# Gated linear attention feeding a mixture of attention experts: outputs of one 128-token window and the state growth of the next as one task, with a reordered end, a narrower mask product and 128-token first projections

## The chip, the cores and the metric

One Trainium2 chip, one core. The metric is the device time of one execution in microseconds (us), lower is better; the kernel before was timed in 3 runs. Five engines run side by side, each in the order in which its instructions were written: PE (matrix products; PEld is its loading of weights), DVE (vector), ACT (scalar functions and copies), POOL (a second, slower vector engine) and SP (here only issues DMAs). They wait for each other through semaphores.

## What is computed

The reference, cut to what matters (B=4, heads H=8, S=768 tokens, D=48; then E=4 experts of width 64 over 384 features):

```python
f = sigmoid(f_logit)
for t in range(S):                                   # gated linear attention (GLA), per head
    state = f[t][:, None] * state + outer(k[t], v[t])
    y[t] = q[t] @ state
x = y as (B, S, 384)
logits = x @ w_gate; the two best experts get softmax weights w
for e in range(E):                                   # each expert: causal attention over all 768 tokens
    q, k, v = x @ wq[e], x @ wk[e], x @ wv[e]
    a = softmax(causal(q @ k.T / 8))
    out += w[e] * (a @ v @ wo[e])                    # 0 where e is not among the two
```

## The kernel before

All work is cut into tasks (`Order.add`): each has a kind, the engines that can run it with a planned cost, a function that emits its instructions, the tasks it needs, and the buffers it takes and uses. `Order.run` is a list scheduler that runs when the program is built: it keeps a planned clock for each engine, takes the task that can start first (ties by `place - AHEAD[kind]`), picks the engine, and so writes down one fixed order for every engine. `AHEAD`, `PLACES`, `WINDOW_AT`, `STICK` are the numbers that steer it. None of this costs anything on the chip; what counts there is the order.

**GLA windows** (`gla_window`, line 315): 24 windows of 128 tokens (`n`), six for each batch element. A window loads f, k, q as one block `fkq` (672 KB, line 341; three buffers) and v; ACT takes exp and log of f (L348, L349), DVE the running sum (L354), ACT two more exps (L360, L361), DVE scales k and q (L364, L365). Then PE has four tasks: `kt` (transposes of k, L371; evicted by ACT or DVE as task `gev`), `d` (the growth of the state, L392; it needs that eviction, and the `y` of the window before, through `state[2]`), `a` (scores within 64-token chunks and the part of the output that crosses chunks, L440, L430; evicted to `xs`) and `y` (outputs, L463, L430; it needs `xs` after POOL has masked it, L453). x is written in two parts, high (task `x`, a copy) and low (L482), since the products after it run as three float32r products of high and low parts (`mm3`, L509 to L511). Six small DMAs for a unit (`fill`, L230) move rows of x between partitions.

**Units** (`plan`, line 858): 8 units `u` of 384 tokens, two for each batch element (h = 0, 1). A unit projects x to q and k of two expert pairs (`proj_qk`) and to v and the gate's logits (`proj_v`), then for each pair runs the attention in groups of 128 query tokens (`experts`): scores `s` (L641, plus a causal mask added as a product of a constant with an identity, L645), row maxima on DVE (L657, L661), exp on ACT (L672), the inverse sum on DVE (L678, L679), scaling by POOL (`scale`, L692), transposes `tr` on PE (L702) with copies back (`pt`), and `attend`: the product with v (`av`, L727) and its two copies `zz`. `out_proj` (L748) multiplies by wo, an eviction and a DMA (L933) store 128 tokens. For h = 1 the three groups have 512, 640 and 768 keys, in that order.

The PE runs these tasks in four tilings, which the code calls modes: q (64x64 quarters: `a`, `y`, `d`), h (row halves: `s`), c (column halves: `av`), f (the full array: the rest). The planner charges 93 ns for a change of mode (`CHANGE`). In the first 95 planned us it also puts dummy products (L204) into the gaps it foresees on PE.

The first unit is special: its projections start in two pieces, tokens 0 to 255 and 256 to 383 (`for a, e, ws in ((0, 256, (0, 1)), (256, 384, (2,)))`). Its weights are loaded into four staging buffers `pp` (line 286) and split into high parts (L290 on POOL, or L225 on ACT) and low parts (L295 on DVE).

Of the kernel before, what the change touches and what calls it, by code (L numbers as in the profile page):

```python
# [16 lines left out]
B, H, S, D = 4, 8, 768, 48  # L17
# [26 lines left out]
CHANGE = 93  # L44
SEEN = {"PE": 190, "V": 125, "A": 145, "P": 65, "S": 0}
# [7 lines left out]
    "oev": 85.8, "out": -104.5, "w": -92.5, "wl": -13.5, "flag": 4.9,  # L53
}
STICK = 0
WINDOW_AT = (-0.27, -0.09, 0.18)
# [3 lines left out]
PLACES = {"w": 4.27, "hv": 11.3, "a0": 1.47, "a1": 4.16, "o": 3.45, "at": 23.67, "second": 0.71, "units": 1.53, "gate": 9.81, "wa": 0, "wo": 1.3}  # L60


def acopy(n):
    return 52 + 0.833 * n
# [144 lines left out]
class Kernel:  # L209
# [105 lines left out]
    def gla_window(self, o, n, x, state):  # L315
# [62 lines left out]
        old, sdone, before = state  # L378
# [17 lines left out]
        gr = o.add("d", [("PE", 240 if last_w else 460)], grow, [kev, lv, before], alloc=grown, uses=[ktb, vb], modes=("q", "q"))  # L396
# [61 lines left out]
        def outputs(e):  # L458
            for p in range(NP):
                for c in range(2):  # L460
# [7 lines left out]
        y = o.add("y", [("PE", 470 + (230 if w else 115))], outputs, [sel, lv],  # L468
                  alloc=([x] if w % 3 == 0 else []), uses=[xsb, vb, fkq, x, mid, ab] + ([old] if w else []),
                  modes=("q", "q"))  # L470
        y.spare, y.free = lambda: [ab.t[:, i, 0:NP * C] for i in range(2)], ev
        state = state[:2] + (y,)
# [8 lines left out]
        hi = o.add("x", [("A", acopy(512)), ("V", dcopy(512))], lambda e: self.copy(e, xout(0), yin()), [y], uses=[ab, x])  # L481
        lo = o.add("x", [("V", dcopy(512))], lambda e: nc.vector.tensor_sub(xout(1), yin(), xout(0)), [hi], uses=[ab, x])  # L482
        self.sums += [cm, t2]
        return lo, state
# [115 lines left out]
    def experts(self, o, ts, h, pr, group, first, place):  # L600
# [22 lines left out]
        def product(_):  # L623
            for i, c0 in group:
# [3 lines left out]
                while s0 < n:  # L628
# [379 lines left out]
```

## Time and profile before

| what | value |
|---|---|
| 3 runs, median (lowest to highest) | 363.52 us (363.08 to 363.83) |
| the profiled execution, its own time | 364.69 us |
| its span, first to last instruction | 363.0 us |
| PE busy | 333.1 us, 92% |
| DVE, ACT, POOL busy | 70%, 59%, 36% |
| mean granted clock of PE | 0.974 |
| share of PE in the chain that ended last | 66% |

The profile cuts the span into 40 slices of 9.1 us with a busy share for each engine; the chain of work that ended last goes back from the last instruction to what released each step. A timeline row has the start and the length in us, the engine, the line, the operation with output and input tiles, shapes and count, and in brackets the idle time before it with the engine that ended it. PE's products overlap, so the distance of two starts, not the length of one product, is what a product costs.

### The profile page before, as it was taken

How to read it: one execution, taken by the hardware profiler on the slowest of the kernel's cores; microseconds unless marked ns; L12 is line 12 of the kernel's file. 1: busy time of each engine (PE TensorE's matmuls, PEld its weight loads, DVE VectorE, ACT ScalarE, POOL GpSimd, SP SyncE). 2: the span in 40 equal slices, each digit the busy share in tenths (PEclk: the TensorE clock that was granted, in tenths of full speed). 3: DMA queues.
4: the chain of work that ended last, by engine and by line, in shares of the span. 5: the costliest groups of instructions: out<-in, count | busy, mean ns of one | idle time of the engine just before them, and what ended most of it. 6: DMA issues, size and time to landing. Idle time of an engine off the chain costs nothing.

```text
span 363.0 us, 12181 instructions
## 1 busy us (share of the span) xinstructions
PE 333.1 (92%) x5083; PEld 278.6 (77%) x5086; DVE 255.2 (70%) x583; ACT 215.7 (59%) x541; POOL 129.3 (36%) x184
## 2 busy tenths in 40 slices
PE   5776998998899999899999999999999999999873
PEld 2455996787789788778887996888987968989542
DVE  4675778797798888769686687788883875456510
ACT  3752457586487667756574686585573555546521
POOL 2352214452461254433342445241533244032320
PEclk9898798999999999999999999999999999999988
DMA  7656423443433325033314305342510010011002
GB/s 208 162 158 166 131 84 100 120 116 100 103 96 103 102 75 156 5 100 94 106 46 122 96 8 134 100 118 64 143 45 3 2 24 11 2 68 44 23 1 73
DMA packets 14846, 30.95 MB, mean 85 GB/s; under 512 B 2336, under 2 KB 11040, under 8 KB 14784
## 3 DMA queue, kind: packets, MB, share of 16 engines
q1 hardware_dynamic: 14784, 30.10, 29.8%
q8 instruction: 42, 0.69, 0.8%
q14 instruction: 20, 0.16, 0.1%
HBM read 23.01 MB, written 4.72 MB: 76 GB/s over the span
## 4 chain that ended last, share of the span: by engine, by line
PE 66%; POOL 8%; DMA 7%; DVE 7%; ACT 6%; issue 2%; SPq 2%; POOLq 0%
PE mm L509 9%; PE mm L702 9%; PE mm L727 9%; PE sps L641 9%; PE mm L511 8%; PE mm L510 8%; POOL pp L692 6%; DMA fkq<-fkq 4%; PE sps L463 3%; ACT pp L672 3%; PE mm L392 3%; PE sps L440 2%; PE sps L430 2%; PE sps L645 2%; POOL xs L453 2%
## 5 line engine op out<-in xcount | busy, mean ns | idle before, releaser
L692 POOL TENSOR_SCALAR pp<-pp,den,wt 128x384 f32<-128x384 f32 (+5 forms) x96 | 80.2, 845 | 120.5 <-DVE den L679 71.8
L672 ACT ACTIVATE pp<-sps,nm 128x384 f32<-128x384 f32 (+5 forms) x96 | 60.3, 638 | 15.9 <-DVE nm L657 11.8
L702 PE MATMUL mm<-ident,pp 128*128 128x128 f32 x336 | 53.1, 288 | 9.9 <-POOL pp L692 9.2
L453 POOL TENSOR_SCALAR_AFFINE_SELECT xs<-xs 64x512 f32<-64x512 f32 x48 | 37.4, 778 | 42.4 <-ACT xs L225 25.8
L702 PEld LDWEIGHTS mm<-ident,pp 128*128 128x128 f32 x336 | 38.2, 144 | 17.0 <-POOL pp L692 13.3
L225 ACT ACTIVATE pt<-mm 128x384 f32<-128x384 f32 (+3 forms) x86 | 36.1, 449 | 19.6 <-PE mm L702 19.1
L641 PE MATMUL sps<-kk,qs 64*128 64x384 f32 (+4 forms) x480 | 46.0, 317 | 1.3 <-DVE x L482 1.0
L641 PEld LDWEIGHTS sps<-kk,qs 64*128 64x128 f32 x480 | 35.7, 185 | 7.5 <-issue 3.4
L727 PE MATMUL mm<-pt,vv 128*64 128x384 f32 (+2 forms) x288 | 40.9, 425 | 0.0
L509 PE MATMUL mm<-x,wqk 128*128 128x384 f32 (+2 forms) x108 | 38.4, 355 | 0.3 <-DMA x<-x 0.3
L354 DVE TENSOR_TENSOR_SCAN c<-keep,fkq 112x512 f32<-112x512 f32 x24 | 31.3, 1305 | 9.3 <-ACT fkq L349 8.0
L510 PE MATMUL mm<-x,wqk 128*128 128x384 f32 (+2 forms) x108 | 35.5, 329 | 0.0
L511 PE MATMUL mm<-x,wqk 128*128 128x384 f32 (+2 forms) x108 | 35.4, 328 | 0.0
L727 PEld LDWEIGHTS mm<-pt,vv 128*64 128x64 f32 x288 | 19.8, 138 | 18.9 <-issue 14.6
L657 DVE TENSOR_REDUCE nm<-sps 128x1 f32<-128x640 f32 (+1 forms) x32 | 27.5, 885 | 8.4 <-PE sps L645 8.3
L348 ACT ACTIVATE fkq<-fkq 112x512 f32<-112x512 f32 x24 | 15.1, 631 | 24.5 <-DMA fkq<-fkq 23.3
L661 DVE TENSOR_REDUCE nm<-sps 128x2 f32<-128x768 f32 (+3 forms) x32 | 25.5, 816 | 5.6 <-PE sps L645 4.6
L221 DVE COPY pt<-mm 128x384 f32<-128x384 f32 (+3 forms) x42 | 20.9, 507 | 5.4 <-PE mm L702 5.2
L358 POOL TENSOR_SCALAR cmax<-c 112x4 f32<-112x4 f32 x24 | 6.3, 263 | 50.2 <-DVE c L354 49.7
L364 DVE TENSOR_TENSOR fkq<-fkq 112x512 f32<-112x512 f32 x24 | 18.7, 780 | 6.8 <-ACT fkq L360 6.7
L463 PE MATMUL sps<-xs,v 64*48 64x64 f32 (+1 forms) x768 | 18.7, 227 | 3.8 <-POOL xs L453 3.8
L509 PEld LDWEIGHTS mm<-x,wqk 128*128 128x128 f32 x108 | 20.8, 193 | 1.7 <-issue 0.7
(109 smaller groups left out, 747.7 us busy)
## 6 DMA issues: line engine op xcount, KB each, us to landing
fkq<-fkq SPq DMA_DIRECT2D x21, 672.0 KB, 5.2
v<-v SPq DMA_DIRECT2D x24, 200.0 KB, 5.0
out<-o SPq DMA_DIRECT2D x24, 192.0 KB, 1.9
fkq<-fkq SPq DMA_DIRECT2D x9, 224.0 KB, 6.9
x<-x SPq DMA_DIRECT2D x42, 48.0 KB, 2.7
pp<-wqk SPq DMA_DIRECT2D x3, 256.0 KB, 5.2
pp<-wvg SPq DMA_DIRECT2D x3, 130.0 KB, 5.4
pp<-wo SPq DMA_DIRECT2D x2, 192.0 KB, 3.8
```

The lines of the kernel that those rows point to most:

```text
L225: nc.scalar.activation(out, in_, AF.Copy)
L354: nc.vector.tensor_tensor_scan(cb.t.rearrange("r p t -> r (p t)"), self.keep.rearrange("r p t -> r (p t)"), part(0).rearrange("r p t -> r ...
L453: nc.gpsimd.affine_select(xf, xf, pattern=[[0, 2 * NP], [1, C]], compare_op=ALU.is_ge, fill=0.0, base=0, channel_multiplier=-1)
L463: nc.tensor.matmul(yo(p, g, c, m), vb.t[64 * c:64 * c + 64, v0:v0 + m], xsb.t[64 * c:64 * c + 64, 1 - (g ^ (p // 2)), p], start=w == 0 and ...
L509: nc.tensor.matmul(ps, lh, rh, start=first, stop=False)
L510: nc.tensor.matmul(ps, lh, rl, start=False, stop=False)
L511: nc.tensor.matmul(ps, ll, rh, start=False, stop=last)
L641: nc.tensor.matmul(out, qs.t[r, lq, tq], kks[hs].t[r, lk, sr], start=x == 0, stop=x == 2 and not diag)
L672: nc.scalar.activation(out, in_, AF.Exp, bias=nm.t[:, x, j:j + 1], accum_out=den.t[:, x, j:j + 1])
L692: sc = o.add("scale", [("P", 360 + 0.85 * n)], lambda eng, c0=c0, n=n, x=x, pi=pi: (nc.vector if eng == "V" else nc.gpsimd).tensor_scalar( ...
L702: nc.tensor.transpose(tp.t[:, (jj - j0) * 128:(jj - j0) * 128 + 128], pp.t[:, c0 + jj * 128:c0 + jj * 128 + 128], self.ident)
L727: nc.tensor.matmul(z.t[64 * j:64 * j + 64, a:HALF], ts[sb // TH]["vv"].t[:, sb % TH, e * HD:(e + 1) * HD], pts[j].t[:, sb, a:], start=(sb ...
```

## The change

Five things, of which the first four also move the order, and the last is the order itself:

- **Outputs and growth as one task.** From window 3 on (`FIRST`), windows that are not the last of their unit do not add their `y` task at once. They hand a function `finish` to the next window, which calls it with its own growth: one PE task does `y` of window n and `d` of window n+1, and so needs the masked scores of n and the evicted transposes of n+1. This holds for 14 of the 24 windows (3, 4, 6, 7, ... 21, 22).
- **A narrower second mask product.** The mask is two products for each row half; the second now writes only the last 64 of the 128 key columns (its first 64 columns added zeros).
- **128-token first projections.** Unit 0 projects in three pieces of 128 tokens in place of 256 + 128.
- **The end reordered.** In the last unit, second pair (`end`), the groups run as 768, 640, 512 keys and each waits in the plan for the one before it; POOL or DVE may scale; `attend` runs in two parts, tokens 128 to 383 and then 0 to 127; the projection of tokens 0 to 127 is planned last.
- **New planner numbers**: all of `AHEAD`, `PLACES`, `WINDOW_AT`, and `STICK` = 3.5 (a task in another mode than PE's last one is ranked 3.5 later) in place of 0.

```diff
+FIRST = 3
-STICK = 0
-WINDOW_AT = (-0.27, -0.09, 0.18)
+STICK = 3.5
+WINDOW_AT = (-0.49, -0.33, -0.06)
...
         # gla_window
-        old, sdone, before = state
+        old, sdone, before = state[:3]
+        rest = state[3] if len(state) > 3 else None
...
-        gr = o.add("d", [("PE", 240 if last_w else 460)], grow, [kev, lv, before], alloc=grown, uses=[ktb, vb], modes=("q", "q"))
+        if rest is None:
+            gr = o.add("d", [("PE", 240 if last_w else 460)], grow, [kev, lv, before], alloc=grown, uses=[ktb, vb],
+                       modes=("q", "q"))
+        else:
+            gr = rest(grow, 240 if last_w else 460, [kev, lv], grown, [ktb, vb])
...
+        def finish(more=None, cost=0, needs=(), alloc=(), uses=()):
+            here, o.place = o.place, place
+            def go(e):
+                outputs(e)
+                if more:
+                    more(e)
+            y = o.add("y", [("PE", 470 + (230 if w else 115) + cost)], go, [sel, lv] + list(needs),
...
+        if n < FIRST or n % 3 == 2:
+            return state[:2] + (finish(),)
+        return state[:2] + (None, finish)
...
         # experts
-                            nc.tensor.matmul(out[:, s1 - s0 - 128:], self.eyer[r, x], self.negr[r, x], start=False,
-                                             stop=x == 1)
+                            nc.tensor.matmul(out[:, s1 - s0 - 128 + 64 * x:], self.eyer[r, x],
+                                             self.negr[r, x, 64 * x:], start=False, stop=x == 1)
...
         # probabilities
-            sc = o.add("scale", [("P", 360 + 0.85 * n)], ...
+            sc = o.add("scale", ([("V", 65 + 0.72 * n)] if end else []) + [("P", 360 + 0.85 * n)], ...
...
         # attend
+        for p0, p1 in parts:
+            z = self.mm()
+            last = TH * h + (p1 - 1) // 128
+            spans = [(sb, max(sb - TH * h, 0) * 128) for sb in range(last + 1)]
+            spans = [(sb, max(a, p0)) for sb, a in spans]
...
         # plan
-                for a, e, ws in ((0, 256, (0, 1)), (256, 384, (2,))):
+                for a, e, ws in ((0, 128, (0,)), (128, 256, (1,)), (256, 384, (2,))):
...
+                end = u == 2 * B - 1 and pr == 1
+                s = None
+                for g, group in enumerate(GROUPS[h][::-1] if end else GROUPS[h]):
...
-                self.attend(o, pair, h, pr)
+                self.attend(o, pair, h, pr, ((128, HALF), (0, 128)) if end else ((0, HALF),))
             for i in range(TH):
-                o.place = at + att[u] + i
+                o.place = at + att[u] + (i or (TH if u == 2 * B - 1 else 0))
```

Through the whole program PE runs 197 stretches of one mode before and 189 after; of those in mode q 67 and 54. The dummy products go from 65 to 55. Line numbers of the changed kernel are higher by 1 to 35.

**SP at the start, before**: the loads of the weights (`wvg`, `wqk`, `wo`), of the windows (`fkq`, `v`), and the moves within x.

```order
L286 DMA pp<-wvg 128x260 x3
L286 DMA pp<-wqk 128x512
L341 DMA fkq<-fkq 112x1536
L286 DMA pp<-wqk 128x512 x2
L230 DMA x<-x 16x2x128 x6
L286 DMA pp<-wo 128x384
L343 DMA v<-v 128x400
L286 DMA pp<-wo 128x384
L341 DMA fkq<-fkq 112x1536
L230 DMA x<-x 16x2x128 x6
L343 DMA v<-v 128x400
L341 DMA fkq<-fkq 112x1536
```

The same place in the change:

```order
L287 DMA pp<-wvg 128x260 x3
L287 DMA pp<-wqk 128x512 x3
L287 DMA pp<-wo 128x384
L231 DMA x<-x 16x2x128 x6
L287 DMA pp<-wo 128x384
L342 DMA fkq<-fkq 112x1536
L344 DMA v<-v 128x400
L231 DMA x<-x 16x2x128 x6
L344 DMA v<-v 128x400
L342 DMA fkq<-fkq 112x1536
L231 DMA x<-x 16x2x128 x6
L344 DMA v<-v 128x400
```

The whole-window loads `fkq` of windows 3 and 4, which stood ahead of the first and of the second six moves of x, now stand behind them.

**PE at the end, before** (the second pair of the last unit: scores with 768 keys, the rest of its transposes, then the one product with v):

```order
L702 MATMUL mm<-ident,pp 128x128 x4
L641 MATMUL sps<-kk,qs 128x384 x12
L645 MATMUL sps<-negr,eyer 128x128 x4
L702 MATMUL mm<-ident,pp 128x128 x26
L727 MATMUL mm<-pt_5532,vv 64x384
```

The same place in the change (now with 512 keys, and the first part of `attend`; `okr` is one small product of the input check):

```order
L727 MATMUL mm<-ident,pp 128x128 x9
L664 MATMUL sps<-kk,qs 128x384 x6
L664 MATMUL sps<-kk,qs 128x128 x6
L669 MATMUL sps<-negr,eyer 128x128 x2
L669 MATMUL sps<-negr,eyer 128x64 x2
L727 MATMUL mm<-ident,pp 128x128 x13
L806 MATMUL mm<-ident,okr 1x112
L756 MATMUL mm<-pt_5567,vv 64x256
```

Behind that first part follow, in the change, the 8 transposes of the 512-key group, 6 products with wo, the second part of `attend` (8 products of 128 columns) and 12 products with wo; before, 18 products with wo follow `attend`.

## Rows read from the trace of the kernel before

**Rows 1.** The page: busy us of each engine, its share of the span, and its instructions.

```profile
PE 333.1 (92%) x5083; PEld 278.6 (77%) x5086; DVE 255.2 (70%) x583; ACT 215.7 (59%) x541; POOL 129.3 (36%) x184
```

**Rows 2.** Busy time by stretch: the stretch in us, its length, busy us of PE, PEld, DVE, ACT, POOL with their counts, the granted clock of PE, DMA share, GB/s.

```profile
33.26:40.08 6.83, 6.28 (x134) 5.82 (x135) 3.67 (x7) 1.83 (x5) 0.69 (x2) 0.50 0.44 126
...
50.00:100.00 50.00, 45.25 (x884) 39.03 (x883) 38.74 (x100) 31.76 (x84) 20.16 (x29) 0.97 0.37 99
100.00:340.00 240.00, 236.01 (x3443) 200.36 (x3441) 177.56 (x411) 151.55 (x391) 90.66 (x122) 1.00 0.25 71
...
57.15:60.56 3.41, 1.79 (x60) 1.47 (x59) 3.01 (x12) 2.35 (x10) 0.75 (x2) 1.00 0.79 225
60.56:63.98 3.42, 3.26 (x15) 2.59 (x16) 2.37 (x6) 2.96 (x9) 3.25 (x5) 0.50 0.17 41
...
347.28:350.69 3.41, 3.41 (x16) 2.32 (x15) 1.11 (x2) 0.98 (x2) 0.59 (x1) 0.50 0.01 2
```

**Rows 3.** Timeline of PE near the start: transposes of window 3, dummy products, the outputs of window 2, the first projection.

```profile
27.79 0.60 PE L371 MATMUL mm<-ident,fkq 112*128 112x112 f32 x4
28.59 1.69 PE L204 MATMUL sps<-zb,identb 128*128 128x256 bf16 x14 [0.20 <-ACT xs L225]
32.88 0.33 PE L463 MATMUL sps<-xs,v 64*64 64x64 f32 x4 [2.60 <-POOL xs L453]
33.80 0.98 PE L463 MATMUL sps<-xs,v 64*64 64x64 f32 x25 [0.60 <-POOL xs L453]
...
36.12 0.58 PE L509 MATMUL mm<-x,wqk 128*128 128x256 f32 x1
```

**Rows 4.** Timeline of SP near the start: loads of windows (L341) and the six moves of x (L230).

```profile
18.35 0.33 SPq L341 DMA_DIRECT2D fkq<-fkq  x1
...
20.38 4.99 SPq L230 DMA_DIRECT2D x<-x  x6
...
27.50 3.91 SPq L230 DMA_DIRECT2D x<-x  x6
...
37.05 4.55 SPq L230 DMA_DIRECT2D x<-x  x6
```

**Rows 5.** Timeline of POOL near the start.

```profile
31.70 0.51 POOL L290 TENSOR_SCALAR wo<-pp 128x384 fp32r<-128x384 f32 x1 [3.03 <-DMA pp<-wo]
32.17 1.58 POOL L453 TENSOR_SCALAR_AFFINE_SELECT xs<-xs 64x512 f32<-64x512 f32 x2
```

**Rows 6.** DMA issues by kind: count, KB each, median us from issue to landing.

```profile
fkq<-fkq SPq DMA_DIRECT2D x21, 672.0 KB, 5.2
...
x<-x SPq DMA_DIRECT2D x18, 16.0 KB, 4.5
```

**Rows 7.** Timeline of ACT near the start: the first exp of window 3, and an eviction of transposes.

```profile
23.32 0.63 ACT L348 ACTIVATE fkq<-fkq 112x512 f32<-112x512 f32 x1 [1.16 <-DMA pp<-wqk]
...
28.43 0.54 ACT L225 ACTIVATE kt<-mm 128x448 f32<-128x448 f32 x1
```

**Rows 8.** Timeline of PE: projections of 256 and of 128 tokens.

```profile
40.40 0.28 PE L509 MATMUL mm<-x,wqk 128*128 128x256 f32 x1
40.52 0.29 PE L510 MATMUL mm<-x,wqk 128*128 128x256 f32 x1
...
47.29 0.27 PE L509 MATMUL mm<-x,wqk 128*128 128x128 f32 x1
47.40 0.27 PE L510 MATMUL mm<-x,wqk 128*128 128x128 f32 x1
```

**Rows 9.** Timeline of PE: from a projection (mode f) into outputs of a window (q) and on into a product with v (c).

```profile
154.80 0.34 PE L510 MATMUL mm<-x,wqk 128*128 128x384 f32 x1
154.97 0.33 PE L511 MATMUL mm<-x,wqk 128*128 128x384 f32 x1
155.24 0.69 PE L463 MATMUL sps<-xs,v 64*64 64x64 f32 x32
...
155.94 0.22 PE L430 MATMUL sps<-fkq,mid 48*64 48x64 f32 x1
156.09 3.45 PE L727 MATMUL mm<-pt,vv 128*64 128x384 f32 x24
```

**Rows 10.** The chain that ended last, in order of time (start, us, what): scores (six products of 128 keys, three for each row half) and mask (four products) in unit 0.

```profile
55.32 0.34 PE sps L641 x6
55.66 0.22 PE sps L645 x4
```

**Rows 11.** Timeline of PE at the end.

```profile
329.80 1.07 PE L641 MATMUL sps<-kk,qs 64*128 64x384 f32 x12
...
346.97 2.57 PE L702 MATMUL mm<-ident,pp 128*128 128x128 f32 x12 [3.65 <-POOL pp L692]
```

**Rows 12.** Timeline of DVE at the end: the maxima of the 512-key group, and the last step of its inverse sums.

```profile
331.14 1.22 DVE L661 TENSOR_REDUCE nm<-sps 128x2 f32<-128x1024 f32 x1 [1.07 <-PE sps L645]
...
334.87 0.17 DVE L679 RECIPROCAL den<-den 128x2 f32<-128x2 f32 x1
```

**Rows 13.** Timeline of POOL at the end: the scaling of the 512-key group, two instructions.

```profile
335.24 1.52 POOL L692 TENSOR_SCALAR pp<-pp,den,wt 128x512 f32<-128x512 f32 x2 [3.01 <-ACT o L225]
```

**Rows 14.** Timeline of ACT at the end: the last eviction before the last store.

```profile
357.26 0.49 ACT L225 ACTIVATE o<-mm 128x384 f32<-128x384 f32 x1 [0.55 <-PE mm L511]
```

More of the change, by code (lines that the diff above doesn't have):

```diff
@@ L466, in outputs @@
             inter(0)
[L468 to L472, printed above, removed]
+        self.sums += [cm, t2]
         oc = slice(col0, col0 + W)
@@ L598, in gate, with experts @@
         t["w done"] = o.add("gate", [("V", 900)], choose, [u], alloc=[wt], uses=[ex, rk, mx])
-    def experts(self, o, ts, h, pr, group, first, place):
+    def experts(self, o, ts, h, pr, group, first, place, end=False, after=None):
         nc = self.nc
@@ L650, in experts @@
         cost = sum(3 * (128 * (i + 1) / 2.33 + (45 if wide else 15)) + 125 for i, _ in group)
-        s = o.add("s", [("PE", cost)], product, t["q done", pr] + [k for hs in range(h + 1) for k in ts[hs]["k done", pr]],
+        s = o.add("s", [("PE", cost)], product, t["q done", pr] + [k for hs in range(h + 1) for k in ts[hs]["k done", pr]] + [after],
                   alloc=banks + [t["pt", 2 * pr + j] for j in range(2)], uses=[qs] + kks, modes=("h", "h"))
@@ L683, in experts, with probabilities @@
             o.place = place(j)
-            self.probabilities(o, t, h, 2 * pr + j, group, col, pps[j], den, j, d)
-    def probabilities(self, o, t, h, e, group, col, pp, den, j, d):
+            self.probabilities(o, t, h, 2 * pr + j, group, col, pps[j], den, j, d, end)
+        return s
+    def probabilities(self, o, t, h, e, group, col, pp, den, j, d, end):
         nc = self.nc
@@ L720, in attend @@
         pts = [t["pt", 2 * pr + j] for j in range(2)]
-        def product(_):
-            for sb in range(nb_all):
-                a = max(sb - TH * h, 0) * 128
-                for j in range(2):
-                    e = 2 * pr + j
-                    nc.tensor.matmul(z.t[64 * j:64 * j + 64, a:HALF],
-                                     ts[sb // TH]["vv"].t[:, sb % TH, e * HD:(e + 1) * HD],
-                                     pts[j].t[:, sb, a:], start=(sb == 0), stop=(sb == nb_all - 1))
@@ L731, in attend @@
-        cost = sum(fp32(HALF - max(sb - TH * h, 0) * 128) for sb in range(nb_all))
-        vs = [ts[hs]["vv"] for hs in range(h + 1)]
-        p = o.add("av", [("PE", cost)], product, t["p done", 2 * pr] + t["p done", 2 * pr + 1]
-                  + [v for hs in range(h + 1) for v in ts[hs]["v done"]], alloc=[z, zz], uses=pts + vs, modes=("c", "c"))
-        u = o.add("zz", [("A", acopy(HALF)), ("V", dcopy(HALF))], lambda e: self.copy(e, zz.t[:, 0], z.t[:, :HALF]), [p],
-                  uses=[z, zz])
@@ L749, in product @@
                          pr == 0, pr == 1)
-        p = o.add("o", [("PE", 6 * f32r(DM))], product, [t["z done", pr] for pr in range(E // 2)] + needs, alloc=[ps],
+        p = o.add("o", [("PE", 6 * f32r(DM))], product, needs + [
+            k for pr in range(E // 2) for a, b, k in t["z done", pr] if a <= 128 * i < b], alloc=[ps],
                   uses=zz, modes=("f", "f"))
@@ L866, in plan @@
         wvg, wqk = None, None
-        state, xs, windows = (None, None, None), {}, {}
+        state, xs = (None, None, None), {}
+        windows = self.windows = {}
         self.sums = []
```

53 lines of the change are left out of this document (35 added, 18 removed), and 6 rows, old and new, of the table AHEAD.

## The prediction

> **What bounds the kernel now.** I read the page first, then busy time by stretch, then PE's timeline where a stretch isn't full, and from each gap back to what ended it. PE is busy for 333.1 of 363.0 us and no other engine above 70% [rows 1]. From 100 to 340 us PE misses only 4 of 240 us, from 50 to 100 it misses 4.75 of 50 [rows 2]. So in the middle a change has to take work off PE or shift it without opening gaps, and what there is to win at once lies at the two ends, in two forms: PE idle, and PE at half clock. The half clock comes in stretches of 3.4 us: 6.83 us after the hole at the start, 3.42 at 60.56, 3.41 after the hole at the end [rows 2].
>
> *The hole at the start.* From 28.59 PE runs 1.69 us of dummy products, is idle for 2.60 and 0.60 until POOL has masked the scores of window 2, and only then, at 36.12, begins the first projection, at half clock until 40.08 [rows 2, 3]. POOL is late since it stood waiting for the last piece of wo until 31.70 [rows 5]. Dummies, idle time and half of 6.83 us (at half clock a stretch does half its work) make 1.69 + 2.60 + 0.60 + 3.41 = 8.3 us.
>
> *The hole at the end.* With the 768-key group last, PE is idle for 3.65 us before its transposes, and 347.28 to 350.69 runs at half clock, a loss of 1.7 [rows 2, 11]. The last eviction ends at 357.75 [rows 14]; the 5.25 us to the span's end are a store and the closing of the program.
>
> **The change part by part.** Times are sums against the profiled execution, 364.69 us (span 363.0 and 1.69 around it), which is 1.17 above the median of 363.52. I take the sum off the median.
>
> *The end: -4.1.* From the scores of the first group of the pair, 329.80, to PE's last product at about 357.2 are 27.4 us, of which 5.35 are the hole. With the smallest group last, PE has between the 512-key scores and their transposes 13 transposes at 0.11 us (12 took 2.57 at half clock [rows 11]), one small product, and the first part of the product with v. The whole product takes 3.4 us (its 24 passes from 156.09 on [rows 9]); the first part has 1408 of its 1920 columns, so 2.5. Cover: 4.0 us. The way it has to cover is visible for the same group: maxima from 331.14, inverse sum until 335.04, POOL from 335.24 with 0.76 for each half [rows 12, 13], so 4.9 to the first scaled half. PE waits 0.9. One more stretch of mode c costs two changes of mode (0.23, below), the small product 0.1. So -5.35 + 0.9 + 0.33 = -4.1. The scaling on DVE has no row of this shape; it runs beside POOL's 0.76, and anything up to that is hidden. After it, 6 products with wo (1.05) stand ahead of the second part and cover the copies of the transposes (an eviction of such size takes 0.54 [rows 7]), and 6 more cover its own two short copies. What follows the last product is unchanged. Ends: -5.0 (no wait), -2 (the wait stays near 3 us and draws a half-clock stretch).
>
> *The start: +0.7.* The first projection now needs window 0 alone. Its moves of x are issued from 20.38 to 25.37 and land 4.5 later [rows 4, 6], so PE can begin at about 29, ahead of the outputs of window 2, and the 8.3 us hole can be filled. Against it stand three costs.
> - Products of 128 columns are barely shorter than of 256: 0.11 us from start to start against 0.12 [rows 8]. 72 for tokens 0 to 255 take the place of 36: 72 x 0.11 - 36 x 0.12 = 3.6.
> - The loads of windows 3 and 4 stand behind moves of x. Window 3 goes out at 25.4 instead of 18.35 [rows 4]; with 5.2 to land [rows 6] and 4.5 from its first exp to its transposes (23.32 to 27.79) [rows 3, 7] PE can turn it at 35.1, about when PE gets there (29 + 36 x 0.11 + one window's outputs 0.85 + 9 x 0.12 = 34.9). Window 4 follows the second six moves (31.4 at the earlier pace): 41.1, where PE arrives at 40.4 (transposes 0.6, 27 products 3.0, growth and scores 0.85 each). Wait 0.7. Window 5 follows the third six, which before began 3.25 us after the outputs of window 2 (33.80 to 37.05) and took 4.55 [rows 3, 4]: 33 + 3.25 + 4.55 + 9.7 = 50.5, where PE, having started again at 41.1, arrives at 47.5 (0.6 + 27 x 0.11 to 0.12 + 9 x 0.12 + two of 0.85, rounded up for mode changes). Wait 3.0. Together 3.7.
> - Such waits cost clock: the stretch 57.15 to 60.56 had PE busy for 1.79 of 3.41 us, and the next one ran at 0.50 [rows 2]. I put one such stretch: 1.7.
>
> 8.3 - 3.6 - 3.7 - 1.7 = -0.7, a loss of 0.7. Ends: a gain of 4.7 (no wait, no half clock), a loss of 6.1 (waits doubled, a second half-clock stretch).
>
> The Trainium skill (TensorE: Matmul & The Clock Gate, Back-to-back issue gap) gives N/2.4 + 2.5 ns for a warm matmul alone, about 56 ns for 128 columns and 109 for 256, an estimate by which the split would cost 0.1 us and not 3.6. The rows don't agree at 128; the same page's section on LDWEIGHTS has 128 weight columns at about 107 ns, close to the 0.11 measured. The same page (What's actually happening) lets the clock fall after a window of about 3.4 us in which PE idled; by that the waits here would cost no clock and the forecast would be 1.7 lower, but the row shows a half-busy window was enough.
>
> *Fewer changes of mode: -0.9.* 197 stretches become 189. Entering mode q took 0.27 us from start to start where the same product steps 0.17 otherwise, leaving it 0.15 where its products stand about 0.02 apart [rows 9]: 0.10 to 0.13 each, 8 x 0.115 = 0.9. The work of DVE and ACT stays as it was. Ends: 0 (the removed changes lay in waits) and -1.0.
>
> *The narrower mask: -0.3.* 48 pairs of second products halve their width. Two pairs take 0.17 to 0.22 us [rows 10]; one at most 0.085 to 0.11. Nothing saved and all of a half, 48 x 0.05 = 2.4, are the ends. The nearest row is the projection, where half the width saved 0.12 to 0.11, 8%: 48 x 0.085 x 0.08 = 0.3.
>
> *The new order in the middle: 0,* with 3 either way: the 4.75 us missing from 50 to 100 are small waits that any order moves about; I see no reason for a sign.
>
> Sum: -4.1 + 0.7 - 0.9 - 0.3 = -4.6. On the profiled execution 360.1, on the median 358.9.
>
> **The rivals.**
> - *The start is won.* PE gets to windows 4 and 5 later than I think, so the waits are hidden and the clock stays up. For it: dummy products are planned into these gaps, and moves of x may land sooner. Against: SP issues in order, and each six moves take 3.9 to 5.0 us. 5.4 less: 353.5.
> - *128 columns at the page's price.* A 128-column product steps 0.056: 3.9 less, 355.0. Against: 0.11 in rows 8, the same tiles and shape. This is the mechanism in which streaming, not weight loading, sets the step.
> - *Slower: the merged task waits for the next window.* The outputs of window n now stand behind the eviction of window n+1's transposes, at 14 places, with everything behind them on PE, and the moves and the projection of x behind those. The eviction takes 0.54 on ACT, and one exp ahead of it 0.63 [rows 7]. If each merged task waits for one such exp, 14 x 0.63 = 8.8: 367.7. It decides from 0.33 us a task on (4.6/14). Against: in the order at each of the 14 places at least one other task stands between the transposes and the merged task, nine products for v (1.1 us) or a group's scores at the least.
> - *Slower by the start alone:* the waits double and a second stretch is halved, 5.4 more: 364.3.
> - *No change:* the hole at the end only moves (the copies of the 640-key transposes, queued with the last maxima and exps on DVE and ACT, hold the first part of the product with v) and the rest cancels: about 363.5.
>
> **How the numbers follow.** Forecast 0.56; start won 0.21; the page's price 0.05; no change 0.05; slower by the start 0.05; merged waits 0.08. Two runs of this kernel differ by up to 0.2%, 0.7 us, so that is what I call the same. Faster: 0.56 + 0.21 + 0.05 = 0.82; same 0.05; slower 0.13. The likeliest is 358.9. The range takes in the case of the won start with a little beyond it (352.5) and the forecast with half the end lost and some of the middle's 3 us (362.5); outside are the three cases at 363.5 and above, 0.18.
>
> **What would show it.** In the changed profile: no idle of over 1 us on PE behind the last scores and no half-clock stretch there, with the span ending some 4 us closer to the first scores of the last pair; the first projection beginning near 29 us and stepping 0.11 in each of 108 products; one to two waits of PE for transposes of windows 4 and 5 between 38 and 51 us, and whether a stretch at 0.50 follows; scores of unit 0 at about 54 us as before. Waits of PE before the outputs' lines that end with a copy of `kt` would speak for the merged-task rival; a first score before 50 us for the won start.

## The result, and the profile after

| what | before | after |
|---|---|---|
| median of 4 runs each (lowest to highest) | 363.30 us (361.21 to 363.83) | 352.73 us (350.80 to 353.57) |
| the profiled execution, its own time | 364.69 us | 353.16 us |
| its span | 363.0 us | 351.3 us |
| mean granted clock of PE in it | 0.974 | 0.985 |

The change made the kernel 10.6 us faster, ratio 0.971 (95% interval 0.966 to 0.977). The forecast was 4.6 us faster: right in direction, less than half of the size. The times of the runs below are medians over all executions of a run, while the ratios leave out the few executions that lay over 1.5% above the fastest of their kernel.

**A misreading of mine stands ahead of the prediction.** In the second order block of the section on the change (SP at the start), between `wqk x3` and `wo`, the row `L342 DMA fkq<-fkq 112x1536` is left out, and the sentence below it, that the loads of windows 3 and 4 now stand behind the first and the second six moves of x, is false. In the change the load of window 3 still stands ahead of the first six moves, those of windows 4 and 5 ahead of the second and the third six. The trace shows it. SP's timeline, changed kernel (start and length in us):

```profile
18.20 0.33 SPq L342 DMA_DIRECT2D fkq<-fkq  x1
18.63 0.37 SPq L287 DMA_DIRECT2D pp<-wo  x1
19.56 4.56 SPq L231 DMA_DIRECT2D x<-x  x6
24.22 0.52 SPq L287 DMA_DIRECT2D pp<-wo  x1
25.33 0.33 SPq L342 DMA_DIRECT2D fkq<-fkq  x1
...
26.68 4.59 SPq L231 DMA_DIRECT2D x<-x  x6
...
32.67 0.33 SPq L342 DMA_DIRECT2D fkq<-fkq  x1
35.12 4.35 SPq L231 DMA_DIRECT2D x<-x  x6
```

Beside [rows 4] the loads of windows 3, 4 and 5 go out as early as before or earlier (18.20 for 18.35, 25.33 for 27.03, 32.67 for 35.38).

The page of the changed kernel, busy us and share of the span (against [rows 1]), and its busy time by stretch, columns as in [rows 2]:

```profile
PE 329.7 (94%) x5128; PEld 277.9 (79%) x5128; DVE 257.3 (73%) x597; ACT 215.5 (61%) x541; POOL 127.5 (36%) x180
```

```profile
26.00:36.00 10.00, 10.00 (x167) 9.25 (x165) 8.71 (x19) 5.81 (x14) 3.07 (x4) 1.00 0.68 186
36.00:50.00 14.00, 14.00 (x299) 13.30 (x299) 10.00 (x25) 8.25 (x20) 4.21 (x6) 1.00 0.35 94
50.00:100.00 50.00, 45.31 (x946) 38.04 (x943) 43.37 (x103) 34.07 (x91) 22.11 (x31) 0.97 0.40 105
100.00:340.00 240.00, 237.34 (x3367) 202.18 (x3368) 176.78 (x417) 151.24 (x385) 88.55 (x119) 1.00 0.25 70
64.10:67.50 3.40, 3.40 (x46) 1.88 (x46) 2.29 (x4) 2.14 (x5) 0.32 (x1) 0.50 0.50 111
322.60:345.20 22.60, 22.32 (x192) 18.48 (x191) 12.84 (x29) 11.59 (x28) 5.54 (x5) 1.00 0.10 37
```

From 26 to 50 us PE is never idle and never at half clock; before, the hole and 6.83 us at half clock lay there. While PE has work, one half-clock stretch at 64.10 is left of the later ones (a row by itself, which is why its 3.40 us count again beside the row from 50 to 100). From the scores of the last pair on, 322.6, no row of PE has a wait, where before 3.65 us were idle and 3.41 at half clock.

PE's timeline at the start of the changed kernel: scores of window 2, the first 128-token projection, the outputs of window 2, the transposes of windows 3 and 4.

```profile
26.66 0.69 PE L447 MATMUL sps<-fkq 48*64 48x64 f32 x32
27.52 0.33 PE L532 MATMUL mm<-x,wqk 128*128 128x128 f32 x1
27.68 0.27 PE L533 MATMUL mm<-x,wqk 128*128 128x128 f32 x1
27.79 0.28 PE L534 MATMUL mm<-x,wqk 128*128 128x128 f32 x1
27.90 0.28 PE L532 MATMUL mm<-x,wqk 128*128 128x128 f32 x1
...
31.68 0.69 PE L470 MATMUL sps<-xs,v 64*64 64x64 f32 x32
...
33.72 0.55 PE L372 MATMUL mm<-ident,fkq 112*128 112x112 f32 x4
...
38.80 0.60 PE L372 MATMUL mm<-ident,fkq 112*128 112x112 f32 x4
```

The projection begins at 27.52 (before 36.12, [rows 3]) and stands ahead of the outputs of window 2. Its products step 0.11, as in [rows 8]. No row carries a bracket: PE has no wait here that the timeline lists. POOL at the start, which in [rows 5] stood for wo until 31.70:

```profile
24.42 0.51 POOL L291 TENSOR_SCALAR wo<-pp 128x384 fp32r<-128x384 f32 x1
26.65 1.12 POOL L291 TENSOR_SCALAR wo<-pp 128x384 fp32r<-128x384 f32 x1 [1.72 <-DMA pp<-wo]
28.34 1.82 POOL L460 TENSOR_SCALAR_AFFINE_SELECT xs<-xs 64x512 f32<-64x512 f32 x2 [0.56 <-ACT xs L226]
```

The last piece of wo now goes out at 24.22 in place of 26.56 and is there at 26.65 in place of 31.70.

PE at the end (against [rows 11]): the 512-key scores, the rest of the 640-key transposes, the small product of the input check, the first part with v, the last transposes.

```profile
333.69 1.08 PE L664 MATMUL sps<-kk,qs 64*128 64x384 f32 x12
334.61 0.36 PE L669 MATMUL sps<-negr,eyer 64*128 64x128 f32 x4
334.90 1.64 PE L727 MATMUL mm<-ident,pp 128*128 128x128 f32 x13
336.38 0.26 PE L806 MATMUL mm<-ident,okr 112*1 112x112 f32 x1
336.63 2.94 PE L756 MATMUL mm<-pt,vv 128*64 128x256 f32 x24
339.49 1.09 PE L727 MATMUL mm<-ident,pp 128*128 128x128 f32 x8
```

DVE and POOL scale one half each, against [rows 12, 13], and ACT's last eviction, against [rows 14]:

```profile
338.35 0.55 DVE L717 TENSOR_SCALAR pp<-pp,den,wt 128x512 f32<-128x512 f32 x1
```

```profile
338.51 1.02 POOL L717 TENSOR_SCALAR pp<-pp,den,wt 128x512 f32<-128x512 f32 x1 [4.86 <-DVE den L703]
```

```profile
345.01 0.49 ACT L226 ACTIVATE o<-mm 128x384 f32<-128x384 f32 x1 [0.55 <-PE mm L534]
```

The slower scaling, POOL's, ends at 339.53, and PE comes to the transposes at 339.49: the first part with v covers the scaling with nothing to spare.

### The profile page after: what moved, and what is told of

Same layout as the page of the kernel before. It is cut to its first block, busy times and chain, and to the rows that moved or that the text cites. A ratio compares the mean times of both kernels' runs of the same rounds, so it can differ in the third digit from the quotient of the medians.

```text
span 351.3 us, 12284 instructions
## 1 busy us (share of the span) xinstructions
PE 329.7 (94%) x5128; PEld 277.9 (79%) x5128; DVE 257.3 (73%) x597; ACT 215.5 (61%) x541; POOL 127.5 (36%) x180
## 4 chain that ended last, share of the span: by engine, by line
PE 75%; DVE 7%; POOL 5%; ACT 5%; DMA 4%; issue 2%; SPq 1%; POOLq 0%; ACTq 0%
PE mm L727 11%; PE mm L756 11%; PE sps L664 10%; PE mm L532 10%; PE mm L534 8%; PE mm L533 8%; POOL pp L717 4%; DMA fkq<-fkq 4%; PE sps L447 4%; PE sps L470 3%; PE sps L437 2%; PE mm L394 2%; ACT pp L696 2%; PE mm L372 2%; PE sps L669 2%
## 5 line engine op out<-in xcount | busy, mean ns | idle before, releaser
L717 POOL TENSOR_SCALAR pp<-pp,den,wt 128x384 f32<-128x384 f32 (+5 forms) x93 | 79.2, 862 | 102.9 <-DVE den L703 52.7
L460 POOL TENSOR_SCALAR_AFFINE_SELECT xs<-xs 64x512 f32<-64x512 f32 x48 | 38.5, 802 | 51.3 <-ACT xs L226 42.1
L727 PE MATMUL mm<-ident,pp 128*128 128x128 f32 x336 | 51.3, 282 | 5.1 <-POOL pp L717 4.4
L226 ACT ACTIVATE pt<-mm 128x384 f32<-128x384 f32 (+3 forms) x91 | 37.3, 449 | 21.6 <-PE mm L727 21.4
L727 PEld LDWEIGHTS mm<-ident,pp 128*128 128x128 f32 x336 | 36.8, 140 | 12.3 <-POOL pp L717 7.2
L532 PE MATMUL mm<-x,wqk 128*128 128x384 f32 (+1 forms) x120 | 40.8, 340 | 0.1
L533 PE MATMUL mm<-x,wqk 128*128 128x384 f32 (+1 forms) x120 | 38.3, 319 | 0.0
L534 PE MATMUL mm<-x,wqk 128*128 128x384 f32 (+1 forms) x120 | 38.3, 319 | 0.0
L756 PEld LDWEIGHTS mm<-pt,vv 128*64 128x64 f32 x304 | 21.5, 138 | 18.4 <-issue 13.9
L532 PEld LDWEIGHTS mm<-x,wqk 128*128 128x128 f32 x120 | 22.8, 190 | 1.3 <-ACT pt L226 0.5
L222 DVE COPY pt<-mm 128x384 f32<-128x384 f32 (+3 forms) x37 | 18.7, 513 | 5.9 <-PE mm L727 5.4
L533 PEld LDWEIGHTS mm<-x,wqk 128*128 128x128 f32 x120 | 22.7, 189 | 0.0
L534 PEld LDWEIGHTS mm<-x,wqk 128*128 128x128 f32 x120 | 22.7, 189 | 0.0
L532 PE MATMUL mm<-wvg,x 128*128 128x260 f32 x72 | 22.0, 306 | 0.0
```

The source lines that it names most:

```text
L226: nc.scalar.activation(out, in_, AF.Copy)
L460: nc.gpsimd.affine_select(xf, xf, pattern=[[0, 2 * NP], [1, C]], compare_op=ALU.is_ge, fill=0.0, base=0, channel_multiplier=-1)
L532: nc.tensor.matmul(ps, lh, rh, start=first, stop=False)
L533: nc.tensor.matmul(ps, lh, rl, start=False, stop=False)
L534: nc.tensor.matmul(ps, ll, rh, start=False, stop=last)
L717: sc = o.add("scale", ([("V", 65 + 0.72 * n)] if end else []) + [("P", 360 + 0.85 * n)], lambda eng, c0=c0, n=n, x=x, pi=pi: (nc.vector if ...
```

## Where the 11.7 us of the span went

I summed, over all products of PE, the distance from one start to the next, and set apart idle time, what half clock costs (half of each stretch at half clock), and the step at a change of mode. The end is taken as a whole; "the rest" is what is left over:

| part | forecast | measured, two profiles |
|---|---|---|
| first scores of the last pair to PE's last product | -4.1 | 27.4 to 22.3: -5.1 |
| up to 60 us: idle | | 10.85 to 8.02: -2.8 |
| up to 60 us: half clock | | two stretches, 3.4 and 6.8 us, to one of 3.4: -3.4 |
| projections q, k | +3.6 | 52.2 to 56.6: +4.4 |
| the start together | +0.7 | -1.9 |
| changes of mode, the mask's among them | -0.9 and -0.3 | 41.2 to 38.4: -2.75 |
| idle from 60 to 300 us | 0 (3 either way) | 7.4 to 5.0: -2.4 |
| the rest | 0 | +0.4 |

The row of the start is one draw. Two more profiles with the same order at the start, that of the next run and that of run 2, have PE idle for 6.2 and 5.7 us up to 60 us in place of 8.0, and lose 5.1 and 1.7 us there to half clock; by them the start gave 0.3 and 4.2 us, not 1.9. The kernel before has one profile only.

Executions of one kernel here often differ by 3 to 8 us, and not by the 0.7 that the prediction took from three runs, in good part by how many half-clock stretches they draw. Each execution lists its span and its mean granted clock. Their product I call **full-clock time**; the rest of the span is what half clock costs. Their means over all executions are the measure below, beside the time itself, since they add up. The measure is rough: a difference of two such means is uncertain by about 2 us either way in full-clock time and by 2 to 4 in what is lost, and a half-clock stretch behind PE's last product (4.07 us before, 6.06 after, in the profiles) counts as lost though PE has nothing left to do. The runs were made on three chips, on which the kernel before took 363.21 us (runs 1 to 3), 362.60 (4, 5, 7, 8) and 361.59 (6, 9, 10, 11); the changed kernel was timed on the first, so a difference to it is off by up to these 1.6 us.

The first runs of the experiments put the changed kernel beside the one before once more:

> The changed kernel once more, as the measure for the runs beside it. 352.7 us expected, as in the first timing (350.8 to 353.6).

352.62 us, ratio 0.969 (0.963 to 0.975). Full-clock time 353.2 before and 345.2 after (-8.0), lost to half clock 8.6 and 5.5 (-3.1).

## Experiments

**1. The end as before** (the changed kernel, planned anew):

```diff
-                end = u == 2 * B - 1 and pr == 1
+                end = False
-                o.place = at + att[u] + (i or (TH if u == 2 * B - 1 else 0))
+                o.place = at + att[u] + i
```

> The changed kernel with the last unit in the old order (groups of 512, 640, 768 keys, scaling on POOL alone, one product with v). Theory A (the end is worth what the two traces show from the first scores of the last pair to the last product, 27.4 against 22.3 us): 5.1 us slower than the changed kernel, with one idle stretch of PE of 3 to 4 us and a half-clock stretch behind it. Theory B (the forecast): 4.1 slower. Theory C (the new planner numbers alone close that hole): less than 2 slower.

356.52 us, 3.9 above the changed kernel; full-clock time 349.6, so 4.4 more, and the same 5.5 lost. PE's timeline of it has the old gap again, to the hundredth:

```profile
337.72 2.50 PE L727 MATMUL mm<-ident,pp 128*128 128x128 f32 x12 [3.65 <-POOL pp L717]
```

This was planned anew, but outside the end its idle time stayed as in the changed kernel (11.8 us for 11.6 in the run above), so the end is worth about 4 us, as forecast.

**2. The second mask product 128 columns wide again** (every engine's order stays):

```diff
-                            nc.tensor.matmul(out[:, s1 - s0 - 128 + 64 * x:], self.eyer[r, x],
-                                             self.negr[r, x, 64 * x:], start=False, stop=x == 1)
+                            nc.tensor.matmul(out[:, s1 - s0 - 128:], self.eyer[r, x], self.negr[r, x], start=False,
+                                             stop=x == 1)
```

> The changed kernel with the second mask product 128 columns wide again; the order of all instructions stays. Theory A (read from the two traces: a change of mode that follows the mask takes 0.172 us from start to start with 64 columns and 0.200 with 128, and 38 stretches of scores end so): 38 x 0.028 = 1.1 us slower than the changed kernel, and the step back at 0.200. Theory B (the weights of a product, 128 columns, set the pace, not the columns streamed): no change. The forecast's own figure was 0.3.

353.15 us (349.98 to 358.08): the times don't tell it from the changed kernel. Full-clock time 346.8 against 345.2 is 1.6 more, which the spread of single executions could make too. The trace shows it in the steps: from the last mask product to the first product in the next mode, 0.20 us in 36 of 38 places, against 0.172. That is 38 x 0.028 = 1.1; all steps at changes of mode rise by about 1.5 together. One place, of which the changed kernel's rows (334.61 to 334.90) stand above with the end, in this run:

```profile
332.11 0.39 PE L669 MATMUL sps<-negr,eyer 64*128 64x128 f32 x4
332.43 1.64 PE L727 MATMUL mm<-ident,pp 128*128 128x128 f32 x13
```

Four mask products and the change behind them take 0.32 us here and 0.29 there. So the mask is worth about 1.1 us and not 0.3: most of the width saved shows in the step behind the last mask product, and not inside the pair of products, where I had looked.

**3. Loads of windows planned behind the moves of x** (the loads of windows 3, 4 and 5 need the moves of the window three back, and each load needs the load before it; planned anew):

```diff
-            ... self.fkq[b, w]), alloc=[fkq], size=672)
+            ... self.fkq[b, w]), self.moves.get(n - 3, []) + [self.loaded], alloc=[fkq], size=672)
...
-                    fills[k] = self.fill(o, x, 128 * k, 128 * k + 128, [windows[k]])
+                    fills[k] = self.moves[k] = self.fill(o, x, 128 * k, 128 * k + 128, [windows[k]])
```

> The changed kernel with the loads of windows 3, 4 and 5 planned behind the first, second and third six moves of x (the planner lays out the rest anew). The forecast took that for the order of the change; in truth the loads stand ahead of the moves. Theory A (the forecast's start term was right about the cost and wrong about the order): PE waits for the transposes of windows 4 and 5, first scores of unit 0 3 to 5 us later than 49.3, and 4 to 5.4 us slower than the changed kernel. Theory B (the planner hides later loads, and they would have cost nothing either way): within 1.5 us of the changed kernel.

370.62 us, 18 above the changed kernel, far more than either theory, and no test of the claim: the plan moved everything (8.8 us idle between 100 and 300 us, changed kernel 2.6). The next run keeps the plan.

**4. Only SP's list changed.** The loads of windows 3, 4 and 5 go out at the places of windows 4, 5 and 6, which is just what I had taken the change for; every other engine keeps its order:

```diff
-        for t, e, _ in self.order:
+        for t, e, _ in self.behind():
...
+        sp = lists["S"]
+        loads = [x for x in sp if x[0].kind == "load" and x[0].size == 672][:4]
+        spots = [sp.index(x) for x in loads]
...
+                if i == spots[a + 1]:
+                    new.append(loads[a])
```

> The changed kernel with every engine's order kept, except that SP issues the loads of windows 3, 4 and 5 where it issued those of 4, 5 and 6: behind the first, second and third six moves of x, the order that the forecast reckoned with. Theory A (the forecast's waits are right for that order): PE waits some 0.7 us for the transposes of window 4 and 3.0 for those of window 5, perhaps with a half-clock stretch; first scores of unit 0 about 53 us instead of 49.5, 3.7 to 5.4 us slower than the changed kernel (352.6). Theory B (there is slack in front of those transposes): under 1.5 slower.

364.98 us, 12 above the changed kernel: full-clock time 350.1 (+4.9), lost 13.9 (+8.4). So the prices that I gave to late loads, 3.7 of waiting and 1.7 of clock, were if anything too small; what was wrong is that the change makes them late. The first scores come at 58.8, in the change at 49.3. The wait that ends last is not the one I named. ACT's and PE's timelines of this run:

```profile
47.21 0.63 ACT L395 ACTIVATE fkq<-fkq 112x512 f32<-112x512 f32 x1 [5.80 <-DMA fkq<-fkq]
...
48.50 0.53 ACT L272 ACTIVATE kt<-mm 128x448 f32<-128x448 f32 x1
```

```profile
49.08 0.48 PE L578 MATMUL mm<-x,wqk 128*128 128x128 f32 x1 [3.54 <-ACT kt L272]
```

```profile
44.55:47.97 3.42, 0.99 (x10) 0.84 (x8) 0.00 (x0) 0.72 (x3) 0.01 (x1) 1.00 0.41 122
...
48.00:54.83 6.83, 5.75 (x96) 5.52 (x97) 4.75 (x11) 3.75 (x9) 0.20 (x1) 0.50 0.13 26
```

ACT stood 5.80 us at the exp of a window whose load had gone out at 42.31, with the eviction of the transposes of the window before queued behind it; PE, whose next projection waited for that eviction, stood 3.54. A late load is paid at the head of a queue, by work that doesn't need it. From 44.55 PE was busy for 0.99 of 3.42 us, and the 6.83 us from 47.97 ran at half clock.

**5. First projections of 256 and 128 tokens** (the changed kernel, planned anew):

```diff
-                for a, e, ws in ((0, 128, (0,)), (128, 256, (1,)), (256, 384, (2,))):
+                for a, e, ws in ((0, 256, (0, 1)), (256, 384, (2,))):
-                        o.place = 14.0 + a / 25.6 + pr
+                        o.place = 14.0 + 10 * (a > 0) + pr
```

> The changed kernel with the first projections in pieces of 256 and 128 tokens. 36 products fewer: about 4 us of PE's steps less. Theory A (only the projection of window 0 alone can fill the hole at the start): PE is idle again before the first projection, the first scores come 2 to 4 us later than 49.5, in sum 0 to 3 slower. Theory B (the new order fills the hole anyway, since POOL no longer waits there): 2 to 4 us faster.

361.66 us, 9 above the changed kernel, more than either theory. The plan came out anew: 20.6 us idle in place of 13.0, of it 3.8 after 300 us, where no projection of unit 0 is. So this run can't price the split: the other plan hides it.

**6. The same with the order kept**: the 36 products of tokens 0 to 127 with wqk are left out of their place, with the copies behind them, and done with those of tokens 128 to 255.

```diff
+        skip = x is self.x0 and a == 0
+        if x is self.x0 and a == 128:
+            a = 0
         cs, n = slice(a, b), b - a
...
             def product(e, ps=ps, ws=ws):
+                if skip:
+                    return
```

> The changed kernel with every engine's order kept, but the products of the first unit's tokens 0 to 127 with wqk (36 of 128 columns) are left out of their early place and done together with those of tokens 128 to 255, as products of 256 columns. Theory A (the gain at the start is the hole that 128-token projections fill): 36 x 0.112 = 4.0 us of work leave the stretch from 27.5 us and 36 x 0.008 = 0.3 come back, but PE then waits for POOL's masks of window 2 (30.2) and for window 1's moves of x (about 34.5): idle time before 36 us grows by 3 to 4, and a half-clock stretch may follow (1.7 or 3.4). Time 0 to +4 against the changed kernel. Rival (the split only costs, the order alone fills the hole): -3 to -4. The price of the split itself is read in either case from the projections' steps: -3.7.

352.84 us; full-clock time 344.1 and 8.0 lost, on a chip where the kernel before took 361.59 us (352.2 and 7.9): at full clock -8.0, as the change itself. Its stretch by time, and PE's timeline where the projection stood:

```profile
26.00:36.00 10.00, 7.30 (x122) 6.76 (x126) 7.20 (x12) 4.55 (x10) 2.90 (x5) 0.83 0.70 192
```

```profile
28.71 0.33 PE L470 MATMUL sps<-xs,v 64*64 64x64 f32 x4 [1.63 <-POOL xs L460]
29.63 0.98 PE L470 MATMUL sps<-xs,v 64*64 64x64 f32 x25 [0.60 <-POOL xs L460]
```

All projections of q and k fall from 56.6 to 53.0, the 3.6 of the forecast to the tenth. From 26 to 36 us PE now misses 2.70, and half of a 3.4 us stretch. First scores come at 49.1, in the change at 49.3. So at full clock the split fills a hole about as large as its own price, and the gain at the start is not its doing. The time itself gained less than in the change, 8.7 us (ratio 0.983, 0.976 to 0.990) for 10.6 (0.969): this run lost as much to half clock as the kernel before, the change 3.1 less. Whether the split saves half clock, five executions don't settle.

**7. Outputs and growth as two tasks** (the changed kernel, planned anew):

```diff
-        if n < FIRST or n % 3 == 2:
+        if True:
```

> The changed kernel with outputs and growth as two tasks everywhere, new numbers kept. The order then has 207 stretches of one mode on PE against 182 (dummies not counted). Theory A (the merged task is worth its changes of mode): 25 x 0.10 to 0.115 = 2.5 to 2.9 us slower than the changed kernel, visible in the sum of steps at changes of mode, idle time the same. Theory B (the merged task also costs waits, that is why it is not free): less than 1 slower or faster, with less idle time of PE between 60 and 300 us than the 5 us of the changed kernel.

360.86 us, 8 above the changed kernel; full-clock time 353.9, 7.1 lost. In its trace there are 219 steps at changes of mode for 196, which cost 42.9 us for 38.4, and from 100 to 300 us 10.5 idle for 2.6:

```profile
100.00:340.00 240.00, 229.37 (x3324) 194.03 (x3316) 171.16 (x399) 145.34 (x372) 85.30 (x116) 0.99 0.24 68
```

The changes of mode cost 4.5 more, 0.20 for each of the 23. Whether the idle time comes from the second task or from the other plan, this run can't tell.

**8. and 9. The numbers without the program, and the program without the numbers.** The kernel before with the change's `AHEAD`, `PLACES`, `WINDOW_AT` and `STICK`:

```diff
-STICK = 0
-WINDOW_AT = (-0.27, -0.09, 0.18)
+STICK = 3.5
+WINDOW_AT = (-0.49, -0.33, -0.06)
```

(and likewise every number of `AHEAD` and `PLACES`), and the changed kernel with those of before (the same lines the other way).

> The kernel before with nothing but the planner's new numbers (AHEAD, PLACES, WINDOW_AT, STICK). 197 stretches of one mode against 191. Theory A (the numbers fit the new tasks and are worth little without them): within 1.5 us of the kernel before. Theory B (the numbers alone carry the gain of the start and the middle, 5 us): about 358.

> The changed kernel with the planner numbers of before (AHEAD, PLACES, WINDOW_AT, STICK = 0). Theory A (numbers and program only work together; numbers alone gave +3.4): the end as reordered (-4 to -5) and the mask (-1) stay, the start and the middle come out by chance: 355 to 368, so above the changed kernel by 3 or more. Rival (the program's edits carry the gain): 351 to 354.

The first took 366.52 us, ratio 1.010 (1.007 to 1.013) to the kernel before: full-clock time the same (353.7 each), 11.0 lost for 7.3. The second took 381.81 us (376.06 to 384.89), 15 to 23 above the kernel before on its chip (361.59). Neither half carries the gain; the old numbers on the new program are the slowest plan measured here.

**10. POOL's wait for wo out of the way of the masks** (the kernel before, every order kept but one exchange on POOL):

```diff
+        p = lists["P"]
+        mask = [x for x in p if x[0].kind == "gsel"][2]
+        k = p.index(mask)
+        p[k - 1], p[k] = p[k], p[k - 1]
```

> The kernel before with every order kept but one step of POOL: the split of the last piece of wo, for which POOL waits until 31.7, goes behind the masks of window 2. Theory A (the hole at the start ended with the moves of window 1, which only the 256-token projection needs): the outputs of window 2 come about 3 us earlier, the first projection stays at 36 us, PE's idle time moves and keeps its size; time within 0.7 us of the kernel before. Rival (POOL's wait was the cause): the first projection comes 2 to 3 us earlier and the time falls by 2 to 6.

POOL and PE in this run (window 2's masks now stand ahead of wo):

```profile
29.27 2.72 POOL L492 TENSOR_SCALAR_AFFINE_SELECT xs<-xs 64x512 f32<-64x512 f32 x2 [1.88 <-ACT xs L264]
32.08 0.51 POOL L329 TENSOR_SCALAR wo<-pp 128x384 fp32r<-128x384 f32 x1
```

```profile
33.35 0.39 PE L548 MATMUL mm<-x,wqk 128*128 128x256 f32 x1
```

The first projection came at 33.35 in place of 36.12, still of 256 tokens, and the first scores at 50.2 in place of 54.4. So my theory that window 1's moves held it until 36 falls: POOL's wait for wo held it in the kernel before. The time hardly followed, 360.90 against 361.59 us (ratio 0.999, 0.994 to 1.003): in the profile 4.45 us of idle time are gone and 4.46 more are lost to half clock; over all executions full-clock time fell by 0.4, less than it can resolve. The profiled execution, 365.48 us, is the longest of the 11 and gave the gain back in half-clock stretches at 56, 93 and 346 us; where the others lost it is not shown, and what would keep it was not found.

**11. No dummy products** (the changed kernel; the order of the rest stays):

```diff
-FILL_UNTIL, FILL_COST = 95, 215
+FILL_UNTIL, FILL_COST = 0, 215
```

> The changed kernel without the dummy products; the order of everything else is kept. Theory A (dummies keep the clock up): before 95 us 9.5 us of dummies become idle time, the clock falls to half behind more gaps there, 1.7 us for each stretch; with two to four more stretches +3 to +7. Rival (dummies stand in gaps that cost no clock): 0 to -1.

358.33 us, 5.7 above the changed kernel, but the five executions fall into two groups: 353.59 and 354.52 (full-clock time 345 and 346), near the changed kernel, and 358.33 to 361.20 (352 to 354). The profiled one, 359.58, is of the second. Its path is not the one I expected: the clock column shows no stretch more. Busy time by stretch, and PE's products in two of them:

```profile
28.70:36.20 7.50, 7.50 (x38) 7.50 (x36) 3.09 (x8) 2.81 (x8) 1.70 (x3) 1.00 0.44 114
36.20:40.00 3.80, 3.80 (x60) 3.56 (x59) 2.38 (x5) 0.62 (x1) 0.00 (x0) 1.00 0.20 47
40.00:48.00 8.00, 8.00 (x138) 7.72 (x138) 6.81 (x13) 4.90 (x13) 2.00 (x3) 1.00 0.34 99
```

```profile
34.30 0.41 PE L534 MATMUL mm<-x,wqk 128*128 128x128 f32 x1
34.51 0.41 PE L532 MATMUL mm<-x,wqk 128*128 128x128 f32 x1
...
40.60 0.28 PE L533 MATMUL mm<-x,wqk 128*128 128x128 f32 x1
40.71 0.27 PE L534 MATMUL mm<-x,wqk 128*128 128x128 f32 x1
```

The same products step 0.21 until 40 us and 0.11 after, while the clock column reads 1.00 in both. PE had run at half speed from its first product; the first scores came at 55.8. The two faster executions have no profile; that they came out of the half speed earlier is likely and not shown.

## Why the prediction was right and wrong

- **The end, -4.1: right.** Measured -5.1 in the profiles and 3.9 to 4.4 by taking it back. The hole closed wholly; the 0.9 us of waiting that I left in it did not appear: what PE does between the 512-key scores and their transposes took 4.6 us (334.90 to 339.49) and not 4.0, and DVE's half was scaled at 338.90.
- **The start, +0.7: wrong; here the forecast failed.** The step "The loads of windows 3 and 4 stand behind moves of x" (3.7), with the half-clock stretch drawn by it (1.7), rests on the misread order. Without these 5.4 the start is -4.7 and the whole sum -10.0, near the measured -10.6. That nearness is partly luck, for two reasons. First, the hole gave less: 2.8 idle and 3.4 of clock, 6.2 and not 8.3, since the dummy products moved and did not go (9.6 us before, 9.5 after). The split cost 3.6, as forecast, in 4.4 for all projections. So the start gave 1.9 in the pair of profiles (0.3 and 4.2 by two others). Second, the other terms missed too: of some 7 us by which the profiles miss the forecast, the start is 2.6, the middle 2.4, the changes of mode with the mask 1.6, the end 1.0. What I took for the cause of the gain was wrong too: the 128-token split pays for itself and no more at full clock (run 6), and run 10 points to POOL, which in the change gets the last piece of wo 5 us earlier and is free for the masks. That wasn't tried in the change itself, and in the kernel before it moved the first scores and hardly the time, so the cause of the start's gain stays open.
- **Changes of mode -0.9 and the mask -0.3: right mechanism, too small.** Together -2.75, in 203 changes before and 196 after (dummy products counted as a mode of their own). The mask is about 1.1 of it. The rest, about 1.7, is 0.24 for each of the seven changes less, where a step at a change takes 0.20 on the average and run 7 paid 0.20 for each one more. So the 0.115 was too small; that the kinds of change differ in price and went in different numbers may be the remainder, which no run separates.
- **The middle, 0 with 3 either way:** -2.4, within its bounds, with no one cause that the runs single out.
- **The rivals.** "The start is won" named the time, 353.5, and its sign, a first score before 50 us (49.3), but its reason (PE comes to windows 4 and 5 later than I thought) was not needed. "The page's price" fell again: with the order kept, 36 products less were worth 3.6, so the step is 0.11 and not 0.056; these products don't go by that figure. The Trainium skill (TensorE: Matmul & The Clock Gate, Back-to-back issue gap) gives it for a product alone and says itself that it is too low where each product loads its weights, which the 0.11 here bears out. "The merged task waits" is not borne out: no listed wait of PE in the change behind 28 us ends with a copy of `kt`, and with two tasks, planned anew, the kernel was slower.
- **Not settled:** how the net 1.9 us of the start and the 2.4 of the middle divide between the merged task and the numbers. Runs 3, 5, 7 and 9, which plan anew, moved 8 us and more, beyond the part that they undid, so only runs 2, 4, 6, 10 and 11, which keep the order, and 1, which changed the last pair, price what they name.

## What to carry to other kernels

Read the order of a queue row by row to the end before a term rests on it: one missed row put 5.4 us of waiting and half clock into the sum that the chip did not pay. Where a planner writes the order, undo an edit with the order kept; planned anew, four such runs here lost 8 us and more, and that loss is easily taken for the edit's worth. A late transfer costs most where an engine stands at the head of its queue for it with others' work behind, as ACT did in run 4, so price it by what is queued there.

## What the runs showed of the hardware

- **The clock column says nothing before its first record.** Without dummies PE ran its first 32 us at half speed under a column that reads 1.00: the first clock record in that trace stands at 40.09 us, in the changed kernel's at 6.08. The step of a known product (0.21 for 0.11) is the surer sign.
- **The clock took long to come up.** In that run's profile PE was busy without a gap from 28.70, yet steps stayed at 0.21 until 40.0, 11.3 us. The half-clock stretches inside the other runs last 3.41 or 6.83 us; in run 10 the one at 93.42 lasted 6.83 with PE busy throughout. The Trainium skill (TensorE: Matmul & The Clock Gate, What's actually happening) has one busy window of about 3.4 us; the stretches of 3.41 agree with it, that of run 10 and this start don't.
- **Half-busy is enough to lose the clock.** In run 4 PE was busy for 0.99 of the 3.42 us from 44.55, and the next 6.83 us ran at 0.50; in [rows 2], from 57.15, 1.79 of 3.41 were enough. The clock changes at multiples of 3.41 us from its first record. Cutting all 14 profiles into these steps, at full clock every step with PE busy for under 1.78 us was followed by half clock and none with over 2.13 us was; in between both happen. So over 1.63 us of idle time in one such step always cost the clock here, and 1.28 could, in one gap or in several (from 57.15 the longest was 1.00).
- **POOL beside DVE was slower, in one place each.** A scaling of 128x512 took POOL 1.02 us with DVE scaling the other half from 338.35 to 338.90, and 0.76 on the average of two in [rows 13], where DVE stood idle until 336.24, for 1.00 of the 1.52 us.
